# Attention and a gated feed-forward block on one core: scores ahead of the values in every step, more steps split into two parts, and a weight conversion spread over more steps

## The chip, the core and the metric

The kernel runs on one core of a Trainium2 chip. A core has five engines with an instruction queue each: TensorE (PE, matrix products into PSUM), VectorE (DVE), ScalarE (ACT), GpSimd (POOL) and SyncE (SP), which here only issues DMAs. The metric is the device time of one execution in microseconds. The kernel before took 986.49 us, the median of 3 runs (986.08 to 987.1).

## The reference

```python
def _attn_ref(q, k, v):                      # q, k, v: (4, 8, 1152, 64), float32
    q_pool = q.reshape(B, H, S // 2, 2, D).mean(axis=3)
    scores = (1.0 / np.sqrt(D)) * np.matmul(q_pool, k.transpose(0, 1, 3, 2))
    scores = scores - np.max(scores, axis=-1, keepdims=True)
    attn = np.exp(scores)
    attn = attn / (np.sum(attn, axis=-1, keepdims=True) + 1e-09)
    return np.matmul(attn, v)

def _moe_ref(x, w_in, w_out, s, b):          # x: (2304, 512); w_in (512, 2048), w_out (2048, 512)
    h = x @ w_in
    r = np.maximum(h, 0.0)
    return (s * (r * r) + b) @ w_out
```

There are 32 heads of attention, each with 576 pooled queries, 1152 keys and a head size of 64. Their result, regrouped to 2304 rows of 512, goes through the feed-forward block. The weights arrive in 64-bit floating point.

## The kernel before

**Steps.** The 32 heads make 16 pairs. A head's 1152 keys are 9 blocks of 128 (`j`), so a pair is 18 steps and the attention is 288 steps `n`; below, step 7 is the step with `n % 18 == 7`, steps 0 to 8 are the even head's, 9 to 17 the odd head's, and step 20 is step 2 of the next pair. In each step PE gets four score products `s` (L482, 128 keys by 576 queries into two PSUM banks; two such tiles take turns), one or two units of the maxima of a coming pair (`m`, L452: a product into PSUM, then a DVE reduction `pm`, L453; the units of a pair run 15 steps ahead), and the value products of three steps before (`o`). Everything is in float32 accuracy: fp32r operands in two parts (a high part and a remainder), or one whole fp32 product.

**The three kinds of step.** `KIND` says for each of the 18 steps how the weights `exp(s)` reach the value product. `w` (whole): one exponential on ACT (`pe`, L486), and two whole fp32 products (L514, which the trace shows as four). `v` (split, on DVE): two exponentials (`ph`, L491, rounded, and the full value written back over `s`, L494), a subtraction `pl` on DVE (L497), and six fp32r products (L520, L522, L524: high weights by high values `vv`, by low values `vl`, and low weights `pl` by high values). `g` is the same with the full value in its own buffer `pe` and the subtraction on POOL. `ORD` is a table of nine strings: the order of scores (`s`), maxima (`f`) and value products (`v`, six parts) in PE's queue within a step, by the block that the values are at.

**The end of a head.** Behind a head's last value product (in step 11 for the even, step 2 for the odd head) `finish` puts four copies of 64x288 on ACT (`xu`, L540, and `l`, L541), which empty the two `o` banks before the next head's first value product.

**The shift and the loads.** When the last maximum of a head has been reduced (`c`, L464), ACT issues two small DMAs that write it into the head's query layout `qq` (L467, L468). SP's queue is in order: key and query loads `kraw`, `qraw` for a later pair (L346, L354), the layout of a head into `kk`, `qq` (L400 to L403, "lay"), and the values `vf` of the next head (L359). POOL turns `vf` into `vv` (L210) and `vl` (L427) in steps 7 and 16 (`VS`), and prepares the pair after the next: `qs` (L408, the sum of query neighbours), `kh`, `qh`, `qz` (L210, the rounded parts), the remainders into `kT` (L415) and `qT` (L416), at the steps that `PREP` names. POOL, too, works in order.

**Weights.** `conversions` turns the 64-bit weights into two fp32r parts, by a chain of operations on ACT, DVE and POOL (`s0` to `s5`), each put a number of ticks behind the start by `STA` (in the attention, one tick a step, pairs 10 to 13) and by `STB` (in the feed-forward block). Three of its operations stand in a row on DVE (L159, L161, L162: clamp, shift, combine). In the feed-forward block PE runs `h = x w_in` (L268), DVE makes `gl` from it (L282), and PE runs `y` (L295).

Of the kernel before, what the change touches and what calls it, by code (L numbers as in the profile page):

```python
# [27 lines left out]
AHEAD = 15  # L28
PB, PE = 4, 3

ORD = ("svfvvvfvv",) * 8 + ("vvfvvvfvs",)
KB = 384


KIND = "vwvgvwgvwgvwvwvwvw"

PP = (("ka", 0), ("kb", 0), ("ha", 0), ("hb", 1), ("qs", 1), ("qt", 1), ("qm", 2), ("qh", 2), ("qz", 2), ("kl", 2), ("ql", 3), ("l0", 7))
PREP = (("ka", 10), ("qs", 10), ("kb", 11), ("ha", 11), ("hb", 12), ("qt", 12), ("kl", 13), ("qm", 14), ("qh", 14), ("qz", 14), ("ql", 15), ("l0", 0), ("l1", 9))
LR = 13
LD = 1  # L40
VS = (7, 16)
XT = (1, 2, 3, 5, 8)
SW = (3, 9)
CB, CP = 274, 18
WB = (7, 11)
STA = (0, 4, 6, 9, 11, 13)
STB = (0, 2, 3, 5, 5, 8)
MO = (2, 3, 6)
XS = (1, 2)
DEPTH = 4  # L50
# [2 lines left out]
def f32(ap):  # L53
    return ap.bitcast(F32)
# [3 lines left out]
def attention_moe_kernel(ctx: ExitStack, tc: tile.TileContext, q, k, v, w_in, w_out, s_in, b_in, out):  # L58
# [49 lines left out]
    def conversions(pool, stage, f0, f1, bufs, stages, psum=None):  # L108
# [30 lines left out]
        def narrow(i):  # L139
            _, hi, lo, name = chunks[i]  # L140
# [16 lines left out]
            def s1():  # L157

                nc.vector.tensor_scalar(out=hm, in0=hm, scalar1=W_MIN, scalar2=W_MAX, op0=ALU.max, op1=ALU.min)  # L159

                nc.vector.tensor_scalar(out=biti, in0=hmi, scalar1=0x07FFFFFF, scalar2=3, op0=ALU.bitwise_and, op1=ALU.logical_shift_left)  # L161
                nc.vector.scalar_tensor_tensor(out=fulli, in0=top, scalar=-0x40000000, in1=biti, op0=ALU.bitwise_and, op1=ALU.bitwise_or)  # L162

            def s2():
# [11 lines left out]
                nc.gpsimd.tensor_tensor(out=lo, in0=A, in1=R, op=ALU.add)  # L176
                done(i)

            for at, fn in zip(stages, (s0, s1, s2, s3, s4, s5)):
                later(at, fn)  # L180

        def split(i):
            _, hi, lo, _ = chunks[i]
            st = raw.pop(i)
            nc.scalar.activation(hi, st, AF.Copy)

            def rest():
                nc.gpsimd.tensor_tensor(out=lo, in0=st, in1=f32(hi), op=ALU.subtract)
                done(i)

            later(stages[1], rest)

        def go():
            i = state[0]
# [22 lines left out]
    def later(k, fn):  # L217
        step[1] += 1
        queue.append((step[0] + k, step[1], fn))
# [106 lines left out]
    qm = ap.tile([P, P], F32R, name="qm")  # L326
# [289 lines left out]
    for n in range(NS + LAG):  # L616
        hd, j = divmod(n, NJ)

        at = (n - LAG) % NJ if n >= LAG else None
        products = None  # L620
        units = iter(range((n + AHEAD) * NU // 18, (n + AHEAD + 1) * NU // 18) if n + AHEAD < NS else ())
        for part in ORD[at] if at is not None else "sff":
            if part == "s" and n < NS:
# [12 lines left out]
        if n < NS:  # L636
            p, h = divmod(hd, 2)
            for name, at in PP:
                if n == at:
                    prep.pop(name)()  # L640
            if n == LD:
                load_k(2)
                load_q(2)
            if p + 2 < NPAIR and n % 18 == PREP[0][1]:
                prep = prep_pair(p + 2)
            for name, at in PREP if n >= 9 else ():
                if n % 18 == at and name in prep:
                    prep.pop(name)()
            if p + 2 < NPAIR:
                if n % 18 == LR and p + 3 < NPAIR:  # L650
                    load_k(p + 3)
                    load_q(p + 3)
            if hd + 1 < NH:
                if j == LAG and hd >= 1:
                    load_v(hd + 1)
                if n % 18 in VS:
                    prep_v(hd + 1)
            if n == NS - 3 * NJ:
                moe.fetch(0)
            if n == NS - 2 * NJ:  # L660
                moe.split(0, 1)
            if (CB - n) % CP == 0 and 0 <= CB - n < 7 * CP:
                weights_a()
# [80 lines left out]
```

## Time and profile before

| | |
|---|---|
| median of 3 runs | 986.49 us (986.08 to 987.1) |
| the profiled execution | 984.08 us, of which its span is 982.3 us |
| mean granted clock of PE | 0.993 of full speed |
| busy share of the span | PE 93%, DVE 64%, ACT 55%, POOL 49% |

The profile is of one execution. Its page gives the busy time of each engine, the chain of work that ended last, and the costliest groups of instructions; the trace behind it gives each instruction's start and length, and what ended the idle time ahead of it (`[1.29 <-ACT pe L486]`: 1.29 us idle, ended by ACT's writing of `pe` in line 486). Starts are in microseconds from the start of the span. The attention takes the first 564 us, the feed-forward block the rest.

### The profile page before, as it was taken

The page shows a single profiled execution, that of the slowest core. Times are in us where ns is not written, and L with a number is a line of the kernel's source. Part 1 is how long each engine was busy: PE and PEld are TensorE (multiplying, and loading weights), DVE is VectorE, ACT ScalarE, POOL GpSimd, SP SyncE. Part 2 cuts the span into 40 slices and gives each one's busy share as a digit, 9 for nine tenths or more (in the row PEclk, how much of TensorE's full clock was granted, in tenths as well). Part 3 has the DMA queues.
Part 4 walks back from the last instruction along what each step waited for, and adds up shares of the span by engine and source line. Part 5 has one row for each costly group of instructions (what it writes and reads, how often), then busy time and mean ns, then how long its engine had stood idle before and what let it go on. Part 6 is the DMA issues. An engine that isn't in the chain of part 4 may idle for free.

```text
span 982.3 us, 16025 instructions
## 1 busy us (share of the span) xinstructions
PE 912.4 (93%) x5680; PEld 819.9 (83%) x5680; DVE 629.7 (64%) x1168; ACT 538.9 (55%) x1038; POOL 483.6 (49%) x389
## 2 busy tenths in 40 slices
PE   4989999999999999899889989999999999999998
PEld 2878888888888888788778878789999899999997
DVE  5757777777777777777776477776676663334333
ACT  2756666666666666666666656554444443333332
POOL 7637546744674467568663467665354430110000
PEclk9899999999999999999999999999999999999999
DMA  8788866876697679767753145664534332222211
GB/s 150 139 174 168 164 124 119 175 161 118 125 179 157 115 145 189 160 124 164 175 123 93 42 144 180 204 214 126 172 126 159 107 125 90 65 86 87 86 44 43
DMA packets 255311, 131.15 MB, mean 134 GB/s; under 512 B 203776, under 2 KB 227328, under 8 KB 255232
## 3 DMA queue, kind: packets, MB, share of 16 engines
q1 hardware_dynamic: 244512, 129.62, 55.4%
q10 hardware_dynamic: 10720, 0.52, 0.7%
q8 instruction: 45, 0.74, 0.3%
q14 instruction: 34, 0.28, 0.1%
HBM read 68.68 MB, written 18.87 MB: 89 GB/s over the span
## 4 chain that ended last, share of the span: by engine, by line
PE 76%; DVE 7%; ACT 6%; DMA 4%; issue 3%; ACTq 1%; POOL 1%; SPq 1%; DVEq 0%; POOLq 0%
PE h L268 18%; PE y L295 18%; PE s L482 13%; PE o L514 9%; PE m L452 6%; PE o L522 4%; PE o L524 4%; PE o L520 4%; DVE pl L497 2%; DVE pm L453 1%; ACT l L541 1%; ACT xu L540 1%; ACT pe L486 1%; DMA xr<-xd 1%; ACTq L467 1%
## 5 line engine op out<-in xcount | busy, mean ns | idle before, releaser
L453 DVE TENSOR_REDUCE pm<-m 128x1 f32<-128x384 f32 x432 | 235.6, 551 | 116.7 <-PE m L452 105.0
L482 PE MATMUL s<-qq,kk 128*128 128x288 f32 x1152 | 209.7, 306 | 33.7 <-ACT pe L486 16.8
L268 PE MATMUL h<-x,wih 128*128 128x256 f32 x1152 | 213.5, 283 | 7.5 <-DVE gl L282 6.3
L482 PEld LDWEIGHTS s<-qq,kk 128*128 128x128 f32 x1152 | 172.3, 190 | 52.6 <-ACT pe L486 21.3
L268 PEld LDWEIGHTS h<-x,wih 128*128 128x128 f32 x1152 | 185.7, 189 | 23.1 <-DVE gl L282 7.1
L452 PE MATMUL m<-kh,qz 128*128 128x384 f32 x384 | 168.0, 442 | 7.9 <-DVE pm L453 7.6
L491 ACT ACTIVATE ph<-s 128x576 fp32r<-128x576 f32 x176 | 114.6, 651 | 110.0 <-PE s L482 108.1
L268 PE MATMUL h<-x,wil 128*128 128x256 f32 x576 | 162.2, 282 | 0.0
L276 DVE SCALAR_TENSOR_TENSOR h<-h,sb,r 128x256 f32<-128x256 f32 x144 | 70.4, 489 | 131.0 <-ACT r L285 131.0
L249 POOL TENSOR_TENSOR x<-xr,x 128x1024 fp32r<-128x1024 f32 x27 | 64.9, 2403 | 177.9 <-ACT x L208 177.9
L514 PE MATMUL o<-pe,vf 128*128 128x288 f32 x448 | 144.8, 407 | 0.0
L497 POOL TENSOR_TENSOR pl<-pe,ph 128x576 fp32r<-128x576 f32 x48 | 69.0, 1437 | 138.1 <-ACT pe L494 135.0
L497 DVE TENSOR_TENSOR pl<-s,ph 128x576 fp32r<-128x576 f32 x128 | 96.2, 751 | 37.3 <-ACT s L494 34.3
L285 ACT ACTIVATE r<-h 128x256 f32<-128x256 f32 x144 | 55.6, 386 | 110.4 <-PE h L268 110.2
L295 PE MATMUL y<-wol,gh 128*128 128x512 f32 x288 | 113.1, 393 | 0.0
L295 PE MATMUL y<-woh,gl 128*128 128x512 f32 x288 | 112.9, 392 | 0.0
L295 PE MATMUL y<-woh,gh 128*128 128x512 f32 x288 | 112.7, 391 | 0.0
L268 PEld LDWEIGHTS h<-x,wil 128*128 128x128 f32 x576 | 109.6, 190 | 0.0
L520 PE MATMUL o<-ph,vv 128*128 128x288 f32 x352 | 104.9, 298 | 3.2 <-POOL vv L210 3.2
L522 PE MATMUL o<-ph,vl 128*64 128x288 f32 x352 | 105.2, 299 | 0.9 <-POOL vl L427 0.9
L486 ACT ACTIVATE pe<-s 128x576 f32<-128x576 f32 x112 | 72.9, 651 | 58.7 <-PE s L482 31.5
L524 PE MATMUL o<-pl,vv 128*128 128x288 f32 x352 | 104.4, 297 | 0.3 <-POOL pl L497 0.3
(89 smaller groups left out, 1494.0 us busy)
## 6 DMA issues: line engine op xcount, KB each, us to landing
kk<-kh SPq DMA_DIRECT2D x32, 576.0 KB, 6.0
kraw<-in_k_dram SPq DMA_DIRECT2D x64, 144.0 KB, 3.6
vf<-in_v_dram SPq DMA_DIRECT2D x32, 288.0 KB, 4.8
kk<-kT SPq DMA_DIRECT2D x32, 288.0 KB, 3.7
qq<-qh SPq DMA_DIRECT2D x64, 144.0 KB, 5.8
xr<-xd SPq DMA_DIRECT2D x18, 512.0 KB, 4.1
qraw<-in_q_dram SPq DMA_DIRECT2D x122, 72.0 KB, 2.5
wsti<-in_moe_w_in_dram SPq DMA_DIRECT2D x16, 512.0 KB, 4.9
```

The source lines that it names most:

```text
L268: nc.tensor.matmul(h[:, :TB], st[:, c, :], mv[:, c, :], start=(n == 0), stop=(n == 3 * NC - 1))
L295: nc.tensor.matmul(y[:, :DM], st[:, ts_], mv, start=(first and n == 0), stop=(last and n == 2))
L452: nc.tensor.matmul(ps[:, :KB], st, khs[p][:, e * KB:(e + 1) * KB], start=True, stop=True)
L453: nc.vector.tensor_reduce(out=pms[p][:, col, e:e + 1], in_=ps[:, :KB], axis=AX.X, op=ALU.max)
L482: nc.tensor.matmul(ps[:, a, :HALF], kk[:, i, j * P:(j + 1) * P], qq[:, i, a], start=(i == 0), stop=(i == 1))
L486: nc.scalar.activation(pe, ps[:, :, :HALF], AF.Exp, scale=SCALE)
L491: nc.scalar.activation(ph, ps[:, :, :HALF], AF.Exp, scale=SCALE)
L497: fresh.append(lambda: eng.tensor_tensor(out=pl, in0=full, in1=f32(ph), op=ALU.subtract))
L514: nc.tensor.matmul(o[:, :HALF], vfs[hd % 2][:, j], ph[:, a], start=first, stop=last)
L520: nc.tensor.matmul(o[:, :HALF], vv[:, j], ph[:, a], start=first, stop=False)
L522: nc.tensor.matmul(o[0:D, :HALF], vl[:, j], ph[:, a], start=False, stop=False)
L524: nc.tensor.matmul(o[:, :HALF], vv[:, j], pl[:, a], start=False, stop=last)
```

## The change

- `ORD`: before, eight of nine steps begin with the scores, and the step that ends a head has them last, behind the head's last values. After, all nine begin with the scores, and the first step behind a head's end has a unit of maxima between the scores and the first value product. The head's copies therefore stand behind the exponentials of the step they belong to.
- `KIND`: 8 `v`, 3 `g` and 7 `w` become 8 `v`, 6 `g` and 4 `w`: three whole steps per pair, 48 in all, become split ones with the subtraction on POOL.
- `PREP`: most of the preparation of a pair stands one step earlier (`hb` at 12 as before), `XT`: the scaling `xo` of a finished pair is one tick earlier.
- `conversions`: the operations of `s1` become three stages. In the attention all three are still put at tick 4; in the feed-forward block each has a tick of its own.

```diff
-ORD = ("svfvvvfvv",) * 8 + ("vvfvvvfvs",)
+ORD = ("sfvfvvvvv",) + ("svfvvvfvv",) * 8
-KIND = "vwvgvwgvwgvwvwvwvw"
+KIND = "vgvwvgvgw" * 2
-PREP = (("ka", 10), ("qs", 10), ("kb", 11), ("ha", 11), ("hb", 12), ("qt", 12), ("kl", 13), ("qm", 14), ("qh", 14), ("qz", 14), ("ql", 15), ("l0", 0), ("l1", 9))
+PREP = (("qs", 9), ("ka", 10), ("kb", 11), ("ha", 11), ("qt", 12), ("hb", 12), ("kl", 12), ("qm", 13), ("qh", 13), ("qz", 13), ("ql", 14), ("l0", 0), ("l1", 8))
-XT = (1, 2, 3, 5, 8)
+XT = (1, 2, 3, 4, 8)
-STA = (0, 4, 6, 9, 11, 13)
-STB = (0, 2, 3, 5, 5, 8)
+STA = (0, 4, 4, 4, 6, 9, 11, 13)
+STB = (0, 1, 2, 3, 4, 5, 6, 8)
...
                 nc.vector.tensor_scalar(out=hm, in0=hm, scalar1=W_MIN, scalar2=W_MAX, op0=ALU.max, op1=ALU.min)
 
+            def s1b():
+
                 nc.vector.tensor_scalar(out=biti, in0=hmi, scalar1=0x07FFFFFF, scalar2=3, op0=ALU.bitwise_and, op1=ALU.logical_shift_left)
+
+            def s1c():
                 nc.vector.scalar_tensor_tensor(out=fulli, in0=top, scalar=-0x40000000, in1=biti, op0=ALU.bitwise_and, op1=ALU.bitwise_or)
...
-            for at, fn in zip(stages, (s0, s1, s2, s3, s4, s5)):
+            for at, fn in zip(stages, (s0, s1, s1b, s1c, s2, s3, s4, s5)):
...
-            for name, at in PREP if n >= 9 else ():
+            for name, at in PREP if n >= 8 else ():
```

How the queues stand after this is read from the two programs; the lines of the changed one are four higher from the conversion on. First POOL, in the odd head of pair 6 (head 13), where it turns the head's values (`vv1`, `vl1`) and prepares pair 8 (`qs8` to `qT8`). A name such as `pl13_5` is head 13, block 5, which is step 14. Before:

```order
L210 TENSOR_SCALAR vv1_106<-vf1_104 128x9x64
L427 TENSOR_TENSOR vl1_108<-vf1_104,vv1_106 128x576
L497 TENSOR_TENSOR pl13_0_2887<-pe13_0_2885,ph13_0_2886 128x576
L408 TENSOR_TENSOR qs8_2930<-qraw8_2605 128x576
L210 TENSOR_SCALAR kh8_2931<-kT8_2928 128x576 x2
L415 TENSOR_TENSOR kT8_2928<-kT8_2928,kh8_2931 128x1152
L210 TENSOR_SCALAR qh8_2932<-qT8_2929 128x576
L210 TENSOR_SCALAR qz0_101<-qT8_2929 64x512 x2
L416 TENSOR_TENSOR qT8_2929<-qT8_2929,qh8_2932 128x576
L210 TENSOR_SCALAR vv0_105<-vf0_103 128x9x64
L427 TENSOR_TENSOR vl0_107<-vf0_103,vv0_105 128x576
```

After:

```order
L214 TENSOR_SCALAR vv1_106<-vf1_104 128x9x64
L431 TENSOR_TENSOR vl1_108<-vf1_104,vv1_106 128x576
L412 TENSOR_TENSOR qs8_3058<-qraw8_2741 128x576
L501 TENSOR_TENSOR pl13_1_3070<-pe13_1_3068,ph13_1_3069 128x576
L214 TENSOR_SCALAR kh8_3059<-kT8_3056 128x576 x2
L419 TENSOR_TENSOR kT8_3056<-kT8_3056,kh8_3059 128x1152
L214 TENSOR_SCALAR qh8_3060<-qT8_3057 128x576
L214 TENSOR_SCALAR qz0_101<-qT8_3057 64x512 x2
L501 TENSOR_TENSOR pl13_5_3184<-pe13_5_3182,ph13_5_3183 128x576
L420 TENSOR_TENSOR qT8_3057<-qT8_3057,qh8_3060 128x576
L501 TENSOR_TENSOR pl13_7_3223<-pe13_7_3221,ph13_7_3222 128x576
L214 TENSOR_SCALAR vv0_105<-vf0_103 128x9x64
```

The same preparation now has two more subtractions among it, those of steps 14 and 16, which stand behind `kT`, `qh` and `qz`.

Next ACT at the end of the even head of that pair (steps 10 to 12). Before:

```order
L491 ACTIVATE ph13_1_2911<-s13_1_2906 128x576
L494 ACTIVATE s13_1_2906<-s13_1_2906 128x2x288
L540 ACTIVATE xu6_2940<-o12_0_2767 64x288
L541 ACTIVATE l6_2941<-o12_0_2767 64x288
L540 ACTIVATE xu6_2940<-o12_1_2768 64x288
L541 ACTIVATE l6_2941<-o12_1_2768 64x288
L486 ACTIVATE pe13_2_2951<-s13_2_2946 128x576
```

After:

```order
L495 ACTIVATE ph13_1_3069<-s13_1_3063 128x576
L498 ACTIVATE pe13_1_3068<-s13_1_3063 128x576
L495 ACTIVATE ph13_2_3092<-s13_2_3087 128x576
L498 ACTIVATE s13_2_3087<-s13_2_3087 128x2x288
L544 ACTIVATE xu6_3101<-o12_0_2916 64x288
L545 ACTIVATE l6_3102<-o12_0_2916 64x288
L544 ACTIVATE xu6_3101<-o12_1_2917 64x288
```

The exponentials of step 11 (`s13_2`) stood behind the four copies and now stand ahead of them.

Last, PE at the same place. Before:

```order
L514 MATMUL o12_0_2767<-pe12_8_2870,vf0_103 128x288
L452 MATMUL m7_12_2936<-kh7_2528,qz1_102 128x384
L514 MATMUL o12_1_2768<-pe12_8_2870,vf0_103 128x288
L482 MATMUL s13_2_2946<-qq1_98,kk1_95 128x288 x4
L482 MATMUL s13_3_2955<-qq1_98,kk1_95 128x288 x4
L520 MATMUL o13_0_2964<-ph13_0_2886,vv1_106 128x288
```

After:

```order
L486 MATMUL s13_2_3087<-qq1_98,kk1_95 128x288 x4
L518 MATMUL o12_0_2916<-pe12_8_3018,vf0_103 128x288
L456 MATMUL m7_12_3097<-kh7_2632,qz1_102 128x384
L518 MATMUL o12_1_2917<-pe12_8_3018,vf0_103 128x288
L486 MATMUL s13_3_3110<-qq1_98,kk1_95 128x288 x4
L456 MATMUL m7_13_3117<-kh7_2632,qz1_102 128x384
L524 MATMUL o13_0_3120<-ph13_0_3042,vv1_106 128x288
```

The scores of step 11 moved ahead of the even head's last values, so that two score tiles no longer follow each other at once.

## Rows read from the trace of the kernel before

**Rows 1.** The page: busy time and share of the span by engine.

```profile
PE 912.4 (93%) x5680; PEld 819.9 (83%) x5680; DVE 629.7 (64%) x1168; ACT 538.9 (55%) x1038; POOL 483.6 (49%) x389
```

**Rows 2.** Waits of PE, whole span: waiter, releaser, us in total, times, longest.

```profile
PE s L482 <- ACT pe L486: 16.8, 13, 1.3
PE s L482 <- DVE pl L497: 15.4, 17, 1.5
...
PE m L452 <- DVE pm L453: 7.6, 7, 2.4
PE h L268 <- DVE gl L282: 6.3, 9, 1.4
PE o L520 <- POOL vv L210: 3.2, 1, 3.2
```

**Rows 3.** Timeline of PE, two steps: start, length, engine, line, operation.

```profile
152.19 0.69 PE L482 MATMUL s<-qq,kk 128*128 128x288 f32 x4
...
152.85 0.34 PE L452 MATMUL m<-kh,qz 128*128 128x384 f32 x1
153.03 0.29 PE L522 MATMUL o<-ph,vl 128*64 128x288 f32 x1
...
153.71 0.77 PE L482 MATMUL s<-qq,kk 128*128 128x288 f32 x4
...
155.63 0.69 PE L482 MATMUL s<-qq,kk 128*128 128x288 f32 x4
```

**Rows 4.** Timelines of PE at the ends of two even heads, one pair apart.

```profile
216.18 0.80 PE L482 MATMUL s<-qq,kk 128*128 128x288 f32 x4 [1.29 <-ACT pe L486]
...
248.98 0.79 PE L482 MATMUL s<-qq,kk 128*128 128x288 f32 x4 [1.29 <-ACT pe L486]
```

**Rows 5.** Timelines of ACT and PE at the odd head's end between them.

```profile
230.45 0.40 ACT L540 ACTIVATE xu<-o 64x288 f32<-64x288 f32 x1 [0.80 <-PE o L514]
...
232.08 0.49 ACTq L467 DMA_DIRECT2D qq<-c  x1
...
234.18 0.53 PE L482 MATMUL s<-qq,kk 128*128 128x288 f32 x2 [0.90 <-DVE pl L497]
```

**Rows 6.** Waits of SP's queue over two pairs; its timeline behind one wait.

```profile
SPq L354 <- DMA qq<-c: 17.4, 4, 8.3
...
234.71 1.39 SPq L354 DMA_DIRECT2D qraw<-in_q_dram  x3
...
241.85 0.62 SPq L359 DMA_DIRECT2D vf<-in_v_dram  x1
```

**Rows 7.** Timeline of POOL from the arrival of those values on.

```profile
246.12 0.67 POOL L210 TENSOR_SCALAR vv<-vf 128x576 fp32r<-128x576 f32 x1 [3.65 <-DMA vf<-in_v_dram]
...
248.26 1.41 POOL L497 TENSOR_TENSOR pl<-pe,ph 128x576 fp32r<-128x576 f32 x1
249.63 1.43 POOL L408 TENSOR_TENSOR qs<-qraw 128x576 f32<-128x576 f32 x1
...
252.43 2.65 POOL L415 TENSOR_TENSOR kT<-kT,kh 128x1152 f32<-128x1152 f32 x1
...
255.68 2.31 POOL L210 TENSOR_SCALAR qz<-qT 64x512 fp32r<-64x512 f32 x2
258.07 1.43 POOL L416 TENSOR_TENSOR qT<-qT,qh 128x576 f32<-128x576 f32 x1
...
260.23 1.42 POOL L427 TENSOR_TENSOR vl<-vf,vv 128x576 fp32r<-128x576 f32 x1
```

**Rows 8.** Timeline of PE: the longest wait under the conversion; a window behind it.

```profile
515.01 0.69 PE L452 MATMUL m<-kh,qz 128*128 128x384 f32 x1 [2.40 <-DVE pm L453]
...
516.00:517.00 1.00, 1.00 (x6) 0.99 (x6) 0.63 (x2) 0.00 (x0) 0.29 (x1) 0.50 0.98 214
```

**Rows 9.** Timelines of DVE and PE in the feed-forward block.

```profile
585.15 0.70 DVE L159 TENSOR_SCALAR wi<-wi 128x512 f32<-128x512 f32 x1
...
587.84 0.48 PE L268 MATMUL h<-x,wih 128*128 128x256 f32 x2 [1.23 <-DVE gl L282]
```

More of the change, by code (lines that the diff above doesn't have):

```diff
@@ L189, in rest @@
                 done(i)
-            later(stages[1], rest)
+            later(stages[4], rest)
         def go():
```

## Prediction

> **What bounds the kernel now.** I read the busy shares first: PE is busy 93% of the span, POOL 49% [rows 1]. That says which engine to relieve, not what a relief is worth, so I read PE's waits next: in 982 us PE waits 16.8 us for exponentials ahead of a score product, 15.4 us for DVE's subtraction at the same place, 7.6 us for a maximum's reduction, 6.3 us for `gl` in the feed-forward block and 3.2 us once for `vv` [rows 2]. About 49 us of waits are there to be had, nearly all at the heads' ends. The timelines show why: ACT's four copies stand in front of exponentials there, the next scores wait 1.29 us at an even head's end, and 0.90 us more are lost at an odd one's [rows 4, 5]. A pair takes 248.98 - 216.18 = 32.80 us [rows 4].
>
> Last, the loads that a pair's loop goes through. SP's query loads wait for the two small `c` transfers (17.4 us in two pairs, up to 8.3 at a time [rows 6]); in the pair shown `c` goes out at 232.08 [rows 5], SP goes on at 234.71, issues the odd head's `vf` at 241.85 [rows 6], and POOL, idle for 3.65 us, begins `vv` at 246.12 [rows 7]. So from `c` to `vv` it takes 14.0 us, whatever PE does. From there POOL works without a gap to the end of `vl` at 260.23 + 1.42 = 261.65, 15.5 us [rows 7]. In the kernel before nothing that PE needs soon stands in that row but the `pl` right behind `vl`, and PE does not wait for it. I call the time at which this `vv` begins V.
>
> **PE's work.** A split step with one unit of maxima takes 153.71 - 152.19 = 1.52 us, a whole one with two units 155.63 - 153.71 = 1.92, and a unit costs 153.03 - 152.85 = 0.18 [rows 3]. The difference less one unit is 0.22; the scores ahead of a whole product also take a little longer, which the same difference holds. So a step turned from whole to split gives 0.22 us, 3 x 0.22 = 0.7 us a pair, 10.6 us in 16 pairs. ACT pays a second exponential and POOL a subtraction of 1.37 us (248.26 to 249.63 [rows 7]) for each.
>
> **The heads' ends.** With the scores first and the exponentials ahead of the copies, the wait of 1.29 at the even end and that of 0.90 at the odd one lose their cause. The copies still take 232.08 - 230.45 = 1.63 us of ACT [rows 5], now between the last values and the next first ones, where one unit of maxima covers a little. Of 2.2 us in a pair I let 1.2 stand, and count 1.0 as gone. PE alone would then need 32.80 - 0.7 - 1.0 = 31.1 us a pair (an estimate; 30 to 32).
>
> **POOL's row, the part that decides.** Behind V there now stand, in this order: `vv` and `vl`, 2.14 us (246.12 to 248.26); `qs` and the two `kh`, 2.80 (249.63 to 252.43); the `pl` of step 10, 1.37; `kT` and `qh`, 3.25 (252.43 to 255.68); `qz`, 2.39 (to 258.07); the `pl` of step 14, 1.37 [rows 7]. The sum is 13.3 us. PE wants that `pl` in step 17. If a pair took 31.1 us, the next `c` would come at V + 31.1 - 14.0 = V + 17.1; from the `pl` of step 14 to that `c` PE and DVE have the rest of step 17 (0.5), steps 18 and 19 (1.7 and 1.5) and, from the start of step 20, about 2.9 us to the last reduction, together 6.6 us. So PE would ask for it at V + 10.5, and it comes at V + 13.3: 2.8 us too late, part of them (about 0.9) already at step 13, where the `pl` of step 10 is late behind `qs` and `kh`, some 1.9 at step 17. The period of the loop is 14.0 + 13.3 + 6.6 = 33.9 us. That is 1.1 us more than 32.80, though PE has less to do: the wait for `pl` takes the place of the waits removed. The unsure links are the landing of `vf` (here 4.3 us after its issue [rows 6, 7]; I allow a microsecond either way) and the end of the chain, so 33.0 to 34.9. Step 16's `pl` ends at V + 13.3 + 1.4 + 1.4 = V + 16.1 and is wanted in step 19, about then; it adds nothing of note.
>
> The pairs in which a later pair is prepared and loads are queued in this way are 2 to 13: 12 x 1.1 = **+13.2 us** (bounds +2.4 and +25). Of these, 10 to 13 carry the conversion as well. There POOL has conversion work in the same row, and PE was already held by it before; I take the same 1.1. The attention's conversion keeps its three operations at one tick, so nothing of the 7.6 us for the reduction [rows 2] is counted as won.
>
> **The other parts.** Pair 0 gains the 0.7 of its three steps. In pair 1 the head's `vf` was late and PE waited 3.2 us for `vv` [rows 2]; the layout that delayed it is issued a step earlier, so I take **-3.2** (bounds 0 and -4). Pairs 14 and 15 prepare nothing, POOL has room, and they gain the full 1.7 each: **-3.4**. In the feed-forward block three conversion operations of 0.70 us stood ahead of `gl` on DVE, and PE waited 1.23 us for it [rows 9], 6.3 us in nine such waits [rows 2]; with a tick between them two of the three, 1.40 us, leave its way, more than the wait shown. I take **-6.3** (bounds 0 and -7). The earlier `xo` and the other moved preparations are POOL's work that stays in its order; I cost them at nothing beyond the row above.
>
> The sum is 13.2 - 0.7 - 3.2 - 3.4 - 6.3 = -0.4 us against the profiled 984.08, 983.7. The median of the runs stands 2.4 us over the profiled execution, so I forecast 986 us, and since the ends of the `pl` row allow more on the side of a smaller wait than of a larger one, 985.5.
>
> **A rule against the row.** POOL's row has no gap for 15.5 us while its share of the span is 49% [rows 1, 7]. The Trainium skill, Perfetto Trace Analysis, section Identifying the Most-Contended Engine, says to optimize the engine with the highest occupancy first; by it, work moved from PE to POOL is all gain, which is the first rival's time. The trace speaks against reading it from the span's share alone, since POOL is idle before V and full behind it.
>
> **Rivals.** *The loop does not bind.* If `vf` comes some 3 us sooner, or the preparations slip behind the subtractions without loss, PE's own work sets the pair: 14 pairs x 1.7 = 23.8, pairs 0 and 1 another 0.7 + 3.2 and the feed-forward block 6.3: -34, so about 952 us, and with half of the late `pl` left some 966. For it: POOL is idle half of the time [rows 1]. Against it: `vf` hangs on the `c` transfers, and these on PE's last maxima [rows 5, 6].
>
> *PE's clock falls, slower.* After the one wait of 2.40 us the granted clock was 0.50 in the window shown [rows 8], the 1.2 GHz level; waits of 1.29 us, which come in pair after pair [rows 4], left the mean over the whole span at 0.993. The new wait at step 17 lies between. If it is enough, the steps behind run at half speed for about 3.4 us, which costs 1.7 us a pair, on the path to the next `c`: 12 x 1.7 = 20 us, 1005 us. It decides from a wait of somewhere between 1.3 and 2.4 us at step 17; were the wait there 1.3 or less, it would not come. It is slower than before.
>
> *The late end.* `vf` lands a microsecond later than in the pair shown, since POOL and SP are fuller, and the feed-forward waits stay: +12 and +6, so about 997 to 1003 us.
>
> *The change does not do what it says:* the copies are still ahead of something that PE needs at once, and the heads' ends keep their waits. Then the loop still sets 33.9 us, and the time is the forecast's.
>
> **How the numbers follow.** Chances: the loop as worked out 0.52 (its own range 975 to 996), the loop not binding 0.22, the clock 0.16, the late end 0.10. About 0.2%, or 2 us, is what a measurement of this kernel can tell from no change. Of the forecast's 0.52, 0.24 lies below 984.5, 0.15 within 2 us of 986.5 and 0.13 above. So faster 0.24 + 0.22 = 0.46, same 0.15, slower 0.13 + 0.16 + 0.10 = 0.39. The range must reach to the first rival's time but for its lowest end, and into the clock's: 955 to 1001.
>
> **What would show it.** In the changed kernel's trace PE's waits should move from the scores (L486 in its numbering) to a value product that waits for POOL's `pl` (L528), about 1.9 us at step 17 and 0.9 at step 13 in pairs 2 to 13, with pairs of 33.9 us; `vv` should begin about 14 us behind `c`, POOL have no gap from there to the `pl` of step 14; the last two pairs should be near 31 us; the nine waits for `gl` should be gone. I am wrong if pairs 2 to 9 take 31 us with no wait for `pl`, or if the granted clock is 0.50 behind step 17 in each pair.

## The result, and the profile after

The changed kernel takes 1000.6 us (median of 4 runs, 1000.3 to 1001.87) against 986.73 for the kernel before: a ratio of 1.0143, 95% interval 1.0115 to 1.0171. It is slower by 14 us. The forecast was 985.5 us with a range of 955 to 1001, so the time lies at the upper end of the range and on the wrong side of no change.

The page of the kernel after, busy time by engine: POOL did get the subtractions (from 483.6 us [rows 1] to 549.8), and ACT the second exponentials.

```profile
span 998.4 us, 16537 instructions
PE 921.4 (92%) x5776; PEld 821.1 (82%) x5776; DVE 630.1 (63%) x1168; ACT 564.7 (57%) x1086; POOL 549.8 (55%) x437
```

PE's waits over the whole span (waiter, releaser, us in total, times, longest):

```profile
PE o L528 <- POOL pl L501: 27.4, 23, 2.4
...
PE m L456 <- DVE pm L457: 5.8, 5, 1.4
PE o L526 <- POOL vl L431: 5.2, 6, 0.9
...
PE o L524 <- POOL vv L214: 4.0, 5, 1.5
PE h L272 <- DVE gl L286: 3.9, 6, 1.6
PE s L486 <- DVE pl L501: 3.6, 9, 0.9
```

The waits ahead of the scores, 16.8 and 15.4 us before [rows 2], are down to 3.6. In their place PE waits 27.4 us for POOL's subtraction, 5.2 for `vl` and 4.0 for `vv`. So the edit did what it says at the heads' ends, and a new wait took more than it gave.

One pair shows the loop. PE's timeline in the odd head of pair 6, steps 12, 13 and 17:

```profile
255.48 0.40 PE L524 MATMUL o<-ph,vv 128*128 128x288 f32 x1 [1.10 <-POOL vv L214]
...
256.97 0.34 PE L526 MATMUL o<-ph,vl 128*64 128x288 f32 x1 [0.91 <-POOL vl L431]
...
259.71 0.40 PE L528 MATMUL o<-pl,vv 128*128 128x288 f32 x1 [0.89 <-POOL pl L501]
...
268.10 0.40 PE L528 MATMUL o<-pl,vv 128*128 128x288 f32 x1 [1.61 <-POOL pl L501]
```

The same pair's links on ACT, SP and POOL: `c` sent, SP freed, `vf` issued, `vv` begun, the subtraction of step 14.

```profile
238.99 0.49 ACTq L471 DMA_DIRECT2D qq<-c  x1
...
240.89 1.39 SPq L358 DMA_DIRECT2D qraw<-in_q_dram  x3
...
248.19 0.54 SPq L363 DMA_DIRECT2D vf<-in_v_dram  x1
...
254.75 0.67 POOL L214 TENSOR_SCALAR vv<-vf 128x576 fp32r<-128x576 f32 x1 [5.93 <-DMA vf<-in_v_dram]
...
266.65 1.40 POOL L501 TENSOR_TENSOR pl<-pe,ph 128x576 fp32r<-128x576 f32 x1
```

From `c` to `vv` it is 15.8 us here, where the rows of before gave 14.0 [rows 5, 7]; `vf` needs 6.6 us from its issue to the start of `vv`, not 4.3. From `vv` to the end of that subtraction POOL has no gap: 268.05 - 254.75 = 13.3 us, as worked out. Where the 16.1 us of the span went:

| stretch | forecast | measured |
|---|---|---|
| pairs 2 to 9, eight (32.89 us each before, 34.79 after) | +8.8 | +15.2 |
| pairs 10 to 13, four with the conversion (34.31, 36.46) | +4.4 | +8.6 |
| start to step 2 of pair 2 | -3.9 | -4.0 |
| step 2 of pair 14 to the end of the attention | -3.4 | -1.9 |
| feed-forward block | -6.3 | -1.7 |
| sum | -0.4 | +16.1 |

A pair is counted here from the scores of step 2 to the scores of the next step 2 on PE's timeline, and the attention ends with its last value product. The text ahead of the prediction puts the conversion in pairs 10 to 13; its chain runs once in each of pairs 10 to 15 (in the kernel before, the clamps of pairs 14 and 15 start at 511.14 and 545.88 us).

### The profile page after: what moved, and what is told of

It reads as the page before. It is cut to its first block, busy times and chain, and to the rows that moved or that the text cites. A ratio compares the mean times of both kernels' runs of the same rounds, so it can differ in the third digit from the quotient of the medians.

```text
span 998.4 us, 16537 instructions
## 1 busy us (share of the span) xinstructions
PE 921.4 (92%) x5776; PEld 821.1 (82%) x5776; DVE 630.1 (63%) x1168; ACT 564.7 (57%) x1086; POOL 549.8 (55%) x437
## 4 chain that ended last, share of the span: by engine, by line
PE 58%; POOL 13%; DMA 8%; ACT 8%; DVE 6%; issue 4%; ACTq 1%; SPq 0%; POOLq 0%; DVEq 0%
PE h L272 16%; PE y L299 16%; PE s L486 9%; PE o L524 4%; PE m L456 4%; POOL pl L501 4%; PE o L528 4%; PE o L526 3%; PE o L518 3%; POOL kT L419 2%; POOL qz L214 2%; DMA vf<-in_v_dram 2%; DMA kk<-kh 2%; ACT ph L495 2%; DMA wsto<-in_moe_w_out_dram 2%
## 5 line engine op out<-in xcount | busy, mean ns | idle before, releaser
L457 DVE TENSOR_REDUCE pm<-m 128x1 f32<-128x384 f32 x432 | 233.0, 550 | 128.8 <-PE m L456 124.6
L495 ACT ACTIVATE ph<-s 128x576 fp32r<-128x576 f32 x224 | 145.9, 651 | 133.7 <-PE s L486 114.1
L486 PE MATMUL s<-qq,kk 128*128 128x288 f32 x1152 | 213.8, 308 | 4.1 <-DVE pl L501 3.6
L501 POOL TENSOR_TENSOR pl<-pe,ph 128x576 fp32r<-128x576 f32 x96 | 137.5, 1432 | 104.8 <-ACT pe L498 103.5
L528 PE MATMUL o<-pl,vv 128*128 128x288 f32 x448 | 135.7, 303 | 27.4 <-POOL pl L501 27.4
L456 PE MATMUL m<-kh,qz 128*128 128x384 f32 x384 | 153.5, 409 | 5.9 <-DVE pm L457 5.8
L524 PE MATMUL o<-ph,vv 128*128 128x288 f32 x448 | 138.7, 310 | 12.0 <-issue 4.4
L526 PE MATMUL o<-ph,vl 128*64 128x288 f32 x448 | 134.1, 299 | 5.4 <-POOL vl L431 5.2
L528 PEld LDWEIGHTS o<-pl,vv 128*128 128x128 f32 x448 | 85.7, 191 | 45.9 <-POOL pl L501 35.4
L524 PEld LDWEIGHTS o<-ph,vv 128*128 128x128 f32 x448 | 85.6, 191 | 25.1 <-ACT l L545 8.0
```

What stands on the lines that cost most here:

```text
L456: nc.tensor.matmul(ps[:, :KB], st, khs[p][:, e * KB:(e + 1) * KB], start=True, stop=True)
L457: nc.vector.tensor_reduce(out=pms[p][:, col, e:e + 1], in_=ps[:, :KB], axis=AX.X, op=ALU.max)
L486: nc.tensor.matmul(ps[:, a, :HALF], kk[:, i, j * P:(j + 1) * P], qq[:, i, a], start=(i == 0), stop=(i == 1))
L495: nc.scalar.activation(ph, ps[:, :, :HALF], AF.Exp, scale=SCALE)
L501: fresh.append(lambda: eng.tensor_tensor(out=pl, in0=full, in1=f32(ph), op=ALU.subtract))
L524: nc.tensor.matmul(o[:, :HALF], vv[:, j], ph[:, a], start=first, stop=False)
```

## Experiments

The table has every run: time, ratio to the kernel before with its interval, and the mean length of the pairs.

| kernel | us | ratio | pairs 2 to 9 | pairs 10 to 13 |
|---|---|---|---|---|
| before | 986.7 | | 32.89 | 34.31 |
| after | 1000.6 | 1.0143 (1.0115 to 1.0171) | 34.79 | 36.46 |
| a_ord | 1004.9 | 1.0175 (1.0146 to 1.0204) | 34.56 | 36.39 |
| a_kind | 980.0 | 0.9929 (0.9905 to 0.9952) | 33.37 | 33.45 |
| b_kind | 1004.9 | 1.0171 (1.0149 to 1.0193) | 34.51 | 36.44 |
| a_l0 | 973.5 | 0.9852 (0.9834 to 0.9871) | 31.95 | 35.41 |
| b_l0 | 996.2 | 1.0100 (1.0080 to 1.0120) | 32.80 | 36.34 |
| a_l0_c | 965.2 | 0.9788 (0.9766 to 0.9810) | 31.20 | 35.41 |
| b_kind_c | 1004.8 | 1.0192 (1.0166 to 1.0218) | 34.07 | 37.60 |
| a_kind_l0 | 965.5 | 0.9780 (0.9744 to 0.9817) | 31.37 | 33.03 |
| a_k11 | 962.7 | 0.9757 (0.9723 to 0.9790) | 31.43 | 34.62 |
| a_mix | 957.2 | 0.9686 (0.9645 to 0.9728) | 31.19 | 33.59 |
| a_l0_sta | 970.4 | 0.9834 (0.9803 to 0.9864) | 31.94 | 35.41 |
| best | 958.6 | 0.9707 (0.9668 to 0.9746) | 31.42 | 33.62 |
| best_sta | 953.0 | 0.9654 (0.9622 to 0.9685) | 31.43 | 32.34 |
| mix_sta | 950.8 | 0.9648 (0.9624 to 0.9672) | 31.19 | 32.52 |
| b_conv | 982.5 | 0.9963 (0.9947 to 0.9980) | 33.52 | 34.26 |

### Which part costs: ORD and KIND apart

```diff
 # a_ord: after, with
-ORD = ("sfvfvvvvv",) + ("svfvvvfvv",) * 8
+ORD = ("svfvvvfvv",) * 8 + ("vvfvvvfvs",)
 # a_kind: after, with
-KIND = "vgvwvgvgw" * 2
+KIND = "vwvgvwgvwgvwvwvwvw"
 # b_kind: before, with
-KIND = "vwvgvwgvwgvwvwvwvw"
+KIND = "vgvwvgvgw" * 2
```

> The kernel after with ORD of the kernel before. The loop theory: the last maximum is reduced and c sent 1.0 us behind the start of step 2 instead of 2.84, so the loop is 1.8 us shorter, about 33.0 us a pair where 34.8 was: 8 x 1.8 + 4 x 1.8 = 22 us less, 976 to 983 us. The rival (more work on POOL alone made the kernel slower, ORD is a gain that it hides): without the gain at the heads' ends the time is 1000 us or more.

> The kernel after with KIND of the kernel before (three steps of a pair whole again, no subtraction in POOL's row behind kT and qz). The loop theory: the subtraction that PE waits for is that of step 9, right behind vl, 3.6 us behind the start of vv; the loop is still there through vv, vl and this subtraction: vv 17.6 us behind step 2, next step 2 about 15.8 us later, 33.4 us a pair: 984 to 990 us, no better than the kernel before. The rival (KIND alone is what costs): pairs of 31.9 us and 965 to 972 us.

> The kernel before with KIND of the kernel after, nothing else. The loop theory: c goes out early and vv begins 14.9 us behind step 2; with the preparations at their old steps the subtraction of step 14 stands behind kT but ahead of qh and qz, so its row is some 3 us shorter, ends 10.3 us behind the start of vv and hides. PE keeps the 0.7 us a pair of three whole steps: 32.1 us a pair, 974 to 980 us. The rival (KIND alone is what costs): pairs of 33.5 us or more, 995 us or more.

With either ORD the new KIND makes the kernel slower by some 18 to 21 us (986.7 to 1004.9 by itself; 980.0 to 1000.6 beside the rest of the edit), and the new ORD makes it faster by 4 with the new KIND. Only a_kind went as expected, by its pairs (33.4 us) and, at 980.0, a little better in time; the pairs' mean came out so by luck, since pairs 6 and 7 (36.7 and 34.7 us) hold stretches at a granted clock of 0.50 and the other six have a mean of 32.6. In a_ord `c` did go out 1.85 us sooner and `vv` began 15.8 us behind step 2 instead of 17.6, but PE now waited 31.5 us ahead of scores for DVE's subtraction (0.9 a pair at step 4, which the old ORD brings back, and up to 1.7 at step 15), the pairs gained 0.2 us instead of 1.8, and the rival's time, 1000 us or more, was right. In b_kind I had let the subtraction of step 14 hide and found 32.1 us a pair; it took 34.5, and the rival that I had put at 995 us or more was right. The trace of b_kind shows, at steps 13 to 15 of pair 5, what I had left out, which is the same in a_ord. ACT first, then PE:

```profile
222.41 0.64 ACT L486 ACTIVATE pe<-s 128x576 f32<-128x576 f32 x1
225.10 0.49 ACTq L467 DMA_DIRECT2D qq<-c  x1
225.69 0.56 ACTq L468 DMA_DIRECT2D qq<-c  x1
226.30 0.65 ACT L491 ACTIVATE ph<-s 128x576 fp32r<-128x576 f32 x1 [3.25 <-PE o L520]
...
228.43 0.77 PE L482 MATMUL s<-qq,kk 128*128 128x288 f32 x4 [1.20 <-DVE pl L497]
```

ACT is idle for 3.25 us, 2.4 of them after the scores of step 13 were written at about 223.9: its queue has the even head's two `c` DMAs ahead of that exponential, and these wait for DVE's reduction, which ends at 225.1. In the old KIND step 13 is whole, with one exponential, and the delay is made up; in the new one steps 13 and 14 are split, four exponentials, and the scores of step 15 wait for them. That is a second cost of KIND, which the prediction put at nothing. The Trainium skill, PSUM — Partial Sum Buffer, section Engine vs sequencer instructions, says that the queues of ScalarE, VectorE and GpSimd are strictly first in, first out; the 2.4 us agree.

### Breaking the loop: l0 behind vf

```diff
 # a_l0: after; b_l0: before
-("l0", 0)
+("l0", 4)
```

> The kernel after, with the layout of the next pair's even head (l0) put at step 4 instead of step 0, so that it stands behind the odd head's vf in SP's queue and no longer ahead of it. The theory (a loop from the c transfers over SP's queue, vf, vv and POOL's row to the subtraction of step 14 sets the pair): the five layout DMAs took 5.8 us of SP's queue ahead of vf, so vv begins about 11.7 us behind the start of step 2 instead of 17.6, the subtraction of step 14 ends at 25.0 us where PE asks for it at 27.3, and the waits for pl at steps 13 and 17 go. Pairs 2 to 9 take 31.2 us instead of 34.8, pairs 10 to 13 about 32.7 instead of 36.5: 952 to 957 us. The rival (POOL has too much work, whenever the values come, or the copies at the heads' ends set the pair): the waits stay and the time is 995 to 1002 us.

> The kernel before with l0 at step 4 instead of 0, nothing else. Theory (in the kernel before the loop is hidden by a little: vv begins 14.9 us behind step 2 and PE does not wait for POOL): vv begins some 5 us sooner and pairs 2 to 9 stay at 32.8 us, 34.3 us under the conversion; 983 to 987 us. The rival (the loop was at its limit already): pairs shorter by 1 us or more, 975 us or less.

In a_l0 the waits for `vv`, `vl` and `pl` are gone in pairs 2 to 9, `vv` begins 12.6 us behind step 2 instead of 17.6, and the kernel is 27 us faster: the loop was what made it slow. The size missed by 16 us: in the pairs with the conversion another bound held, and in the others a rest of 0.4 to 1.0 us stayed at step 14. That rest is the ACT queue again (a_l0, pair 4; PE, then ACT):

```profile
181.33 0.77 PE L486 MATMUL s<-qq,kk 128*128 128x288 f32 x4 [0.86 <-DVE pl L501]
...
177.34 0.49 ACTq L471 DMA_DIRECT2D qq<-c  x1
177.92 1.23 ACTq L472 DMA_DIRECT2D qq<-c  x1
179.20 0.65 ACT L495 ACTIVATE ph<-s 128x576 fp32r<-128x576 f32 x1 [2.21 <-DVE pm L457]
```

b_l0 is the control: there `vv` begins 11.4 us behind step 2 instead of 14.9, and the eight pairs take 32.80 us each, the usual 32.8 without the one that took 33.37. So the loop was in the kernel before too, hidden with almost nothing to spare. But b_l0 as a whole is slower by 10 us, which nothing in my expectation had. Eight of them come from pairs 10 to 13 (36.34 against 34.31 us), the rest in that one execution mainly from pairs 1 and 15 and the feed-forward block. In pairs 10 to 13 the earlier `vl` now runs beside the conversion's three DVE operations. In pair 11 of b_l0 (DVE, POOL, PE):

```profile
410.16 0.71 DVE L161 TENSOR_SCALAR wabo<-whmo 128x512 int32<-128x512 int32 x1
410.96 1.71 DVE L162 SCALAR_TENSOR_TENSOR wAo<-wsto,wabo 128x512 int32<-128x512 int32 x1
...
410.67 1.45 POOL L427 TENSOR_TENSOR vl<-vf,vv 128x576 fp32r<-128x576 f32 x1
...
413.19 0.45 PE L452 MATMUL m<-kh,qz 128*128 128x384 f32 x1 [2.39 <-DVE pm L453]
```

In pair 11 of the kernel before, with POOL idle beside them, the same operations take 0.43 and 0.69 us and PE waits 1.09:

```profile
409.11 0.43 DVE L161 TENSOR_SCALAR wabo<-whmo 128x512 int32<-128x512 int32 x1
409.63 0.69 DVE L162 SCALAR_TENSOR_TENSOR wAo<-wsto,wabo 128x512 int32<-128x512 int32 x1
...
410.84 0.44 PE L452 MATMUL m<-kh,qz 128*128 128x384 f32 x1 [1.09 <-DVE pm L453]
```

The Trainium skill, SBUF — State Buffer, section Who interferes with whom, says that a DVE instruction with two SBUF inputs contends with a GpSimd instruction that reads SBUF, and that the port pair they share is an exclusive lock. The combining operation has two such inputs; it began behind `vl` and ended 0.55 us after it, and 0.69 against 1.71 us agrees. PE's waits for this reduction in pairs 10 to 13 are 4.2 us in the kernel before and 9.6 in b_l0. The other 3 us of the eight stand in pairs 11 and 13 (37.1 us each, where 10 and 12 took 35.6), in which the granted clock was 0.50 behind that wait. In pair 14 of the kernel before `vl` ran beside the combining operation already (1.71 us): the one wait of 2.40 us [rows 8] is of this kind.

### The c DMA behind the exponentials

```diff
 # a_l0_c: a_l0; b_kind_c: b_kind
-        later(1, send)
+        later(2 if hd % 2 == 0 else 1, send)
```

> The kernel after with l0 at step 4 (a_l0, 973.5 us), and the c DMAs of the even heads one tick later on ACT's queue. Theory of the queue: the waits of 0.4 to 0.9 us ahead of the scores of step 15 go, 0.75 us a pair in pairs 1 to 9, less in the pairs with conversions: 964 to 968 us. The rival (ACT's four copies and its six exponentials in a row are too much by themselves): the waits stay, 972 to 975 us.

> The kernel before with the new KIND (b_kind), and the c DMAs of the even heads put one tick later on ACT's queue, behind the exponentials of step 13 instead of ahead of them. Theory of the queue (with two exponentials in each of steps 11, 13 and 14, ACT has no slack, and the c DMA at the queue's head, which waits for DVE's reduction, holds the exponentials of step 13 back by about 2.5 us): the wait of 1.2 us ahead of the scores of step 15 goes, 1 to 1.3 us a pair in 14 pairs: 986 to 991 us against 1004.9. The rival (ACT has simply too much to do, or the loop over vf and POOL's row sets these pairs as well): within 4 us of 1004.9.

a_l0_c came out as expected: step 14, which took between 2.0 and 2.7 us, takes 1.67, every pair from 2 to 9 takes 31.20 us, and 8 us are gone. This is the pair that PE sets in the new order, with the stall of step 12 that the next section looks at; the prediction had 31.1 for it, with some of the heads' waits left in. b_kind_c did not: the wait at step 14 went there as well (3.03 to 1.67 us in most pairs), and the time stayed. Its waits of PE beside those of b_kind show where it went; first b_kind, then b_kind_c:

```profile
PE s L482 <- DVE pl L497: 28.6, 29, 1.7
...
PE o L524 <- POOL pl L497: 6.6, 8, 1.3
```

```profile
PE o L524 <- POOL pl L497: 16.2, 12, 2.3
...
PE s L482 <- DVE pl L497: 12.7, 16, 1.3
```

What PE no longer waits for at the scores it waits for at POOL's subtraction: the loop stands close behind the ACT queue, and removing the first alone shows the second. In both kernels it is step 1, 2.82 us in the kernel before, that grows, to 2.8 to 4.3 us in b_kind and up to 6.9 in b_kind_c; there the `pl` of step 16, behind `qh` and `qz`, is late. I had looked at step 14's only. In pairs 10 to 13 of b_kind_c this wait is 2.2 to 2.3 us, and the granted clock is 0.50 behind each of the four, a part of their 37.60 us.

### Is the new KIND worth anything without the loop?

```diff
 # a_kind_l0: a_l0, with
-KIND = "vgvwvgvgw" * 2
+KIND = "vwvgvwgvwgvwvwvwvw"
 # a_k11: a_l0_c, with
-KIND = "vgvwvgvgw" * 2
+KIND = "vgvwvgvgw" + "vgwvvgvgw"
```

> The kernel after with KIND of the kernel before and l0 at step 4: the order of scores, the preparations and the conversion are the new ones, the steps' kinds the old. Theory (the loop over vf costs both, KIND is worth its 0.7 us a pair at most): pairs of 31.1 to 31.5 us without the loop, 32.2 us under the conversion: 952 to 959 us, so that the three split steps a pair have no gain even where the loop does not bind. The rival (the new KIND is worth having once the loop is broken): no better than 973 us.

> The kernel after with l0 at step 4 and the even heads' c DMAs a tick later (a_l0_c, 965.2 us, pairs of 31.20 us without a wait for pl), and in KIND the whole step of the odd head at step 11 instead of 12 (as many of each kind). Theory (the new KIND loses its gain on PE because step 11, whose exponentials stand ahead of the even head's copies on ACT, has two of them where the old KIND has one; step 12 takes 2.78 us where the old one takes 2.04): step 12 falls to 2.1 to 2.2 us, a pair to 30.5 us: 954 to 958 us. The rival (the copies themselves set that stall): 963 to 967 us.

a_kind_l0's time missed (965.5 us; 960.3 in the profiled execution), there by pairs 1 (36.5 us) and 10 to 13 (33.0). But with the old KIND five of the eight pairs from 2 to 9 take 31.17 to 31.20 us, as with the new one in a_l0_c (31.20; a_l0_c has the later `c` DMA as well, which was not tried with the old KIND). So three whole steps less give nothing in the pairs without conversion, though each gives PE about 0.2 us. Step by step, step 12 takes 2.04 us with the old KIND and 2.78 with the new, and without it the pair is 0.7 us shorter with the new one. The reason is on ACT: in step 11, two exponentials stand ahead of the even head's copies where the old KIND has one, and the next head's first value product waits for the copies. a_k11, with the whole step at 11, tests it; ACT of a_k11 at that place:

```profile
235.26 0.65 ACT L490 ACTIVATE pe<-s 128x576 f32<-128x576 f32 x1 [0.54 <-PE s L486]
235.81 0.39 ACT L544 ACTIVATE xu<-o 64x288 f32<-64x288 f32 x1
```

and of a_l0_c:

```profile
232.77 0.65 ACT L495 ACTIVATE ph<-s 128x576 fp32r<-128x576 f32 x1 [0.47 <-PE s L486]
233.32 0.65 ACT L498 ACTIVATE s<-s 128x576 f32<-128x576 f32 x1
233.89 0.40 ACT L544 ACTIVATE xu<-o 64x288 f32<-64x288 f32 x1
```

Step 12 fell to 2.09 us, as expected, but the pair did not: step 3 grew from 2.32 to 2.94 us and step 14 from 1.67 to 1.93, so it takes 31.43. The new wait at step 3 is for ACT's `pe` of that step, ahead of the next scores (3.7 us in eight pairs), which start as that `pe` ends; they seem to use its tile, which no run tests. The 962.7 us can't be told from the 965.2 of a_l0_c by their intervals.

### The pairs with the conversion, and a better version

```diff
 # a_mix: a_l0_c, the old KIND in pairs 10 to 14
+KINDC = "vwvgvwgvwgvwvwvwvw"
-score_step(hd, j, KIND[n % 18])
+score_step(hd, j, (KINDC if 10 <= n // 18 < 15 else KIND)[n % 18])
 # a_l0_sta: a_l0; best_sta: best; mix_sta: a_mix
-STA = (0, 4, 4, 4, 6, 9, 11, 13)
+STA = (0, 4, 5, 6, 7, 9, 11, 13)
 # best: a_mix with the KIND of a_k11
```

> a_l0_c (965.2 us) with the old KIND in pairs 10 to 14, those with the conversion, the new one elsewhere. Theory (there POOL's row is full for most of the pair, and three subtractions more a pair make steps 1, 3 and 17 wait for pl and vl): these pairs go from 35.2 to 32.5 to 33.5 us: 953 to 957 us. The rival (the conversion's three operations on DVE set these pairs, by the 1.7 us at step 9): 961 to 965 us.

> The kernel after with l0 at step 4 (a_l0, 973.5 us), and in the attention too one tick each for the conversion's three DVE operations (STA 4, 5, 6 instead of 4, 4, 4). Theory (three operations in a row on DVE, slowed beside POOL's work from 0.43 and 0.69 to 1.54 and 1.03 us, hold a maximum's reduction back; 1.7 us at step 9 in each of five pairs): this wait goes, 1 to 1.7 us in pairs 10 to 14: 965 to 969 us. The rival (POOL is full there and only moves the wait): 971 to 975 us.

> Both at once: a_l0_c with the whole step at 11 instead of 12 in pairs 0 to 9 and 15, the old KIND in pairs 10 to 14. If both theories hold the gains add, 11 pairs of 0.7 and 5 of 2.2: 944 to 949 us. If POOL or DVE is the bound in the conversion's pairs, 953 to 958 us.

> The kernel best with a tick each for the conversion's three DVE operations in the attention (STA 4, 5, 6). With POOL less full than in a_l0_sta, where the stall only moved to steps 11 and 14, the 1 to 2 us at step 9 should go in part: 940 to 947 us, 2 to 5 us below best. The rival (it moves again): within 2 us of best.

> best_sta (953.0 us) with the whole step of the odd head back at step 12 in pairs 0 to 9 and 15. Theory (with it at 11 the wait of 0.7 us left step 12, and one of 0.6 at step 3 and 0.3 at step 14 came, 31.4 us a pair against 31.2): 950 to 952 us. The rival (no difference that can be told): 952 to 954 us.

In these pairs POOL's row decides first: with three subtractions fewer they are 1.8 us shorter in the mean (a_mix, 35.41 to 33.59). With POOL full, a tick each for the three DVE operations only moved the stall, as the rival to a_l0_sta said (in pair 11 step 9 from 3.2 to 1.5, step 11 from 1.46 to 2.45, step 14 from 2.0 to 2.6 us); its time lies between the two expectations, and the run can't be told from a_l0 by its interval. With POOL relieved it does take step 9 from 3.0 and 3.2 us in the mean to 1.50, gives back 0.4 to 0.7 at step 12, and shortens these pairs by 1.1 to 1.3 us in the mean (33.62 to 32.34, 33.59 to 32.52). Most of that is pair 12 (35.6 to 32.4 us from a_mix to mix_sta), where the wait for the reduction had been 2.25 us in a_mix and the granted clock was 0.50 behind it. The medians fall from 958.6 to 953.0 us and from 957.2 to 950.8; the intervals beside the kernel before overlap, the times themselves do not (954.2 to 958.9 us for a_mix, 949.9 to 953.1 for mix_sta). best itself missed: its gains did not add, since the whole step at 11 gains nothing; best_sta fell as far below it as expected and a little further, and mix_sta came out as expected. mix_sta and best_sta cannot be told apart by their intervals; mix_sta, with 950.8 us, is 3.5% faster than the kernel before and 5% faster than the changed one.

### The conversion's edit alone

> The kernel before with the conversion's edit alone (s1 in three stages, STA with all three at tick 4, STB with a tick each). The prediction's term: the nine waits for gl, 6.3 us, go: 980 us. Theory from the traces so far (a chain that starts late, on a late DMA or a late ACT operation, lets the three operations pile up in DVE's queue again, so that six waits of 3.9 us stay and two for gh come): 984.5 to 986 us, 1 to 2 us less than before.

The kernel before with the three stages and the new STA and STB takes 982.5 us, a ratio of 0.9963 (0.9947 to 0.9980), between the two expectations. In its trace the waits for `gl` are down from 6.3 us to 3.9, and the feed-forward block is 3.4 us shorter. Why not all of it goes is seen in the kernel after (ACT, DVE, PE):

```profile
639.67 0.64 ACT L151 ACTIVATE wo<-wsto 128x512 f32<-128x512 f32 x1 [0.91 <-DMA wsto<-in_moe_w_out_dram]
...
640.34 0.70 DVE L159 TENSOR_SCALAR wo<-wo 128x512 f32<-128x512 f32 x1 [2.68 <-ACT wo L151]
641.07 0.70 DVE L163 TENSOR_SCALAR wo<-wo 128x512 int32<-128x512 int32 x1
641.81 0.70 DVE L166 SCALAR_TENSOR_TENSOR wo<-wsto,wo 128x512 int32<-128x512 int32 x1
...
643.43 0.47 PE L272 MATMUL h<-x,wih 128*128 128x256 f32 x2 [1.57 <-DVE gl L286]
```

The three operations stand at three ticks of the program, but a tick is a place in the queue and not a time. Where the chain begins late, here behind a DMA, DVE finds them waiting and does them in a row again, ahead of `gl`.

## Why the prediction was wrong, point by point

The sum was 16.5 us too low: 6.4 of it in pairs 2 to 9, 4.2 in pairs 10 to 13, 4.6 in the feed-forward block and 1.5 behind step 2 of pair 14.

**The mechanism that decided was the one forecast.** The wait for `pl` took the place of the waits removed, in the pair shown at steps 13 (0.89 us, forecast 0.9) and 17 (1.61, forecast 1.9), through a loop of `c`, SP, `vf` and POOL's row. Taking l0 out of the loop gave 27 us back. POOL's row was 13.3 us, the stretch from `vv` to the next `c` 20.0 us in each of the eight pairs (forecast 13.3 + 6.6 = 19.9), and the pair without the loop 31.20 us (forecast 31.1). Not forecast were the waits at step 12 for `vv` and `vl` themselves, 4.0 and 4.6 us in the eight pairs; where PE waits does not change the loop's length.

**The term that was mis-sized is the link from c to vv**, put at 14.0 us from one pair [rows 5 to 7]. That pair was no odd one: in pairs 2 to 9 of the kernel before the link is 13.4 to 14.8 us, mean 13.9. It grew with the change, to 13.0 to 16.2 us, mean 14.8, and most of that is the time from `vf`'s issue to its landing: 4.1 to 5.7 us before, mean 4.6 (4.2 in the pair that I chose), and 3.6 to 7.0 after, mean 5.2. Its mean is 5.2 to 5.6 us in each of the four kernels with the new KIND and l0 ahead of `vf` (after, a_ord, b_kind, b_kind_c), 4.5 to 4.7 with the old KIND (before, a_kind, b_conv), and 4.2 to 4.6 in all that have l0 behind `vf`. Why the new KIND delays this load is not shown. Before, a late landing cost something in one pair only, and an early one gained nothing. In the loop that binds each counts in full, late or early: with 3.6 us pair 9 took 33.06 us, with 7.0 pair 3 took 36.19. The pairs came out at 34.79 us, at the end of the bounds (33.0 to 34.9) that I had weighted least, having tipped the forecast to 985.5 on the ground that a smaller wait was likelier.

How little was spare before shows in b_conv, whose attention is that of the kernel before: in its profiled execution `vf` took 5.4 and 6.5 us in pairs 5 and 7, and these two took 35.0 and 35.8 us where the others took 32.8 to 33.2. The waits for `pl` that came of it are 0.52 and 1.01 us; the larger part is the granted clock, 0.50 behind both (pair 7; PE, then a stretch in the columns explained below):

```profile
287.74 0.61 PE L528 MATMUL o<-pl,vv 128*128 128x288 f32 x1 [1.01 <-POOL pl L501]
...
288.00:289.00 1.00, 1.00 (x5) 0.90 (x6) 0.05 (x1) 0.00 (x0) 1.00 (x1) 0.50 1.09 291
```

**The pairs with the conversion** were taken with the same 1.1 us. POOL's conversion work lies in the same row: from `vv` to the next `c` it was 22.5 us in pairs 10 to 13 instead of 20.0, while `c` to `vv` was 14.0 as forecast, and these pairs lost 2.15 us each. In pair 11 a conversion operation (1.29 us) stands ahead of `qh`, `qz` and the `pl` of step 14, which ends 14.8 us behind the start of `vv` instead of 13.3:

```profile
427.31 0.88 POOL L214 TENSOR_SCALAR vv<-vf 128x576 fp32r<-128x576 f32 x1 [3.22 <-DMA vf<-in_v_dram]
...
436.43 1.29 POOL L174 TENSOR_TENSOR wRo<-wRo,wabo 128x512 f32<-128x512 f32 x1
...
440.70 1.40 POOL L501 TENSOR_TENSOR pl<-pe,ph 128x576 fp32r<-128x576 f32 x1
```

Pairs 14 and 15, counted at a full gain of 3.4 us because they prepare nothing, carry the conversion too and gave 1.9.

**The conversion in the feed-forward block** was put at -6.3 us and gave -1.7 (-3.4 in b_conv): the edit moves places in a queue, and late chains pile up.

**The edit that was costed at a gain, three whole steps less, is worth nothing here.** The 0.7 us a pair on PE is right as PE's work, but ACT pays for it at step 12 (a_kind_l0, a_k11) and behind the `c` DMAs (b_kind). The prediction named ACT's second exponential and gave it no price; that was the second step that failed, though in the kernel after the loop hid it. It also read the waits of before as nearly all at the heads' ends; 32.2 of the 49.3 us are [rows 2].

**Rivals.** The loop not binding is what pairs 2 to 9 of a_l0_c show once the loop is broken; that its 965.2 us lie within the rival's 952 to 966 is in part chance, since pairs 10 to 13 stayed at 35.4 us for another reason. The clock rival came true in three pairs of twelve. Behind the usual wait at step 17, 1.61 us, the granted clock stays at 1.00, the 2.4 GHz level; behind the two longest, 2.30 and 2.36 us in pairs 10 and 13, it goes to 0.50, the 1.2 GHz level, as behind the 2.40 in the kernel before [rows 8]; and so it does in pair 5 behind two waits at step 12, 0.73 and 0.92 us. The stretches behind the wait of 1.61 us, behind that of 2.30 and behind the two in pair 5, all in the kernel after (stretch, its length, busy time of PE, PEld, DVE, ACT and POOL, granted clock, DMA share, GB/s):

```profile
269.00:270.00 1.00, 1.00 (x10) 0.96 (x9) 0.23 (x1) 0.53 (x1) 1.00 (x2) 1.00 0.00 0
```

```profile
405.86 0.40 PE L528 MATMUL o<-pl,vv 128*128 128x288 f32 x1 [2.30 <-POOL pl L501]
...
407.00:408.00 1.00, 1.00 (x6) 1.00 (x5) 0.00 (x0) 0.19 (x1) 1.00 (x2) 0.50 0.84 131
```

```profile
221.18 0.35 PE L526 MATMUL o<-ph,vl 128*64 128x288 f32 x1 [0.92 <-POOL vl L431]
...
222.00:223.00 1.00, 1.00 (x7) 1.00 (x5) 0.47 (x1) 0.00 (x1) 1.00 (x2) 0.50 1.08 232
```

The length of a wait alone does not decide it: in b_l0 the same wait of 2.39 us comes at step 9 of pairs 10 to 14, and the clock fell behind it in pairs 11, 13 and 14 and not in 10 and 12. In pair 10:

```profile
377.62 0.44 PE L452 MATMUL m<-kh,qz 128*128 128x384 f32 x1 [2.39 <-DVE pm L453]
...
378.00:379.00 1.00, 1.00 (x10) 1.00 (x9) 0.93 (x3) 0.00 (x0) 1.00 (x2) 1.00 1.07 305
```

What does decide it stays open. Nor was the price of 1.7 us a pair right in the loop. Pairs 10 and 13 took 37.2 and 37.4 us where 11 and 12 took 35.6 and 35.7, but 1.1 of these 1.6 us lie between `c` and `vv`, ahead of the wait; from `vv` to the next `c` it is 22.8 against 22.2 us. In pair 5 that stretch is 20.0 us as in the others of pairs 2 to 9: there POOL's row sets the next `c`, and a slower PE waits less for it. Where PE sets the pair, as in b_conv, the slow stretch is paid, with some 1.7 and 2.0 us (an estimate: the two pairs' excess over 32.8 less the waits of 0.52 and 1.01).

The late end, 997 to 1003 us, was given a chance of 0.10 and is nearest to what came: `vf` a microsecond later in the mean of pairs 2 to 9, and most of the feed-forward waits kept (3.9 of 6.3 us). The rule that the prediction weighed against the row (the Trainium skill, Perfetto Trace Analysis, section Identifying the Most-Contended Engine), to relieve the engine with the highest occupancy first, read from the span's share alone would have given the first rival's time; here that reading failed by POOL's gapless row, as the prediction said.

## What to carry to other kernels

Work moved to an engine that is idle half of the time is free only where that engine is idle: look for the stretch in which its queue runs without a gap, and at what opens that stretch. If a transfer opens it and the chain closes on itself, take the mean and the spread of the transfer over all its instances, and leave room for it to grow with the change: in a loop that binds every landing counts, and the mean sets the time. Of an operation added to an in-order queue ask what stands behind it in that queue, DMA issues among it, and price the engine that gets the smallest share of the edit as well.

## What was not expected of the hardware

The same 288 KB load of `vf` lands 3.6 to 7.0 us after its issue within one execution. Layout transfers follow it at once in seven of the eight pairs, late and early ones (in pair 9, the earliest, a weight load stands between), so they don't tell the late ones from the early; the cause stays open. Around the two small `c` DMAs ACT stood idle for 2.2 us (a_l0) and 3.25 us (b_kind), 1.4 and 2.4 of them after the next scores were written: the issue that waits for DVE's result, and the issues' own 1.7 and 1.1 us, stand ahead of the exponentials in ACT's queue. And the conversion's combining operation on DVE took 0.69 us with POOL idle and 1.71 beside POOL's `vl`, while the `pl` subtraction on DVE, which has one input in PSUM, stayed at 0.74 to 0.76 beside POOL's work as without it.
